# Warm-up matmuls that read a ready-made constant in place of a cleared tile, and three more small ones

## The chip, the cores and the metric

The kernel runs on one core of a Trainium2 chip. The metric is device time in microseconds (us) of one execution. A trace of one execution, taken by the hardware profiler, counts its times from the start of that execution's span; the span is about 1.5 us shorter than the device time. All executions quoted here are of the state "fast". Engines are TensorE (PE in the profile; its weight loads are PEld), VectorE (DVE), ScalarE (ACT), GpSimd (POOL) and SyncE (SP); SPq and ACTq are the DMA queues that SyncE and ScalarE feed. In the views, `arena` is the kernel's own block of on-chip memory and `PS` the accumulator banks that TensorE writes; the weights and x are loaded from HBM, the chip's main memory. A load "lands" when its semaphore says that it is complete.

## The reference, cut to what matters

A layer norm of x (2048 tokens of 512, bf16) feeds two branches whose results are added to x: a diagonal state-space model (a product with B, a scan over tokens, a product with C) and a gated MLP, `(gelu(xn @ w_gate) * (xn @ w_up)) @ w_down`, with a hidden size of 1376. The first thing that TensorE can do of real use is to transpose the first centred tiles of x and multiply them by the first columns of `w_gate` and `w_up`.

## The kernel before: the parts that matter

The kernel builds a list of operations with their buffers, and a scheduler orders them on each engine. TensorE and SyncE keep the order in which they were written down. Before the first real work TensorE runs dummies: seven matmuls of 512 columns and two of 128, then four of 128 between pieces of real work.

```python
half = V(lambda e: e.memset(HALF.ap, 0.5), ...)
wrm = S.order_behind(V(lambda e: e.memset(WRM.ap, 0.0), ...), half)   # the tile the dummies read
...
ld_x0(0)                                        # first x tile, SyncE's queue
S.order_behind(ld_x0(1, "scalar", [wrm]), ...)  # ScalarE's queue, behind wrm
ld_wg0(0, "sync")                               # w_gate columns 0-383, rows 0-255
S.order_behind(ld_wg0(1, "scalar", [wrm]), ...) # rows 256-511
ld_x0(2)
ld_w(WU, WUc, ins["B_w_up"], 0)                 # w_up columns 0-383
ld_x0(3)
...
nwarm = 7
wrm4 = WRM.ap.unsqueeze(1).broadcast_to([128, 4, 128])
def fwarm(e, wb=wb):                            # line 913 of the profile
    for _ in range(nwarm):
        ins_ = e.matmul(PS[wb]..., WRM.ap, wrm4, start=True, stop=True)
PE(fwarm, ..., [WRM], [BANK[wb]], "warm")
def fill(n):                                    # line 920
    ... e.matmul(PS[fb][:, 0:128], WRM.ap, WRM.ap, ...) n times
...
fill(2)
cent_T(0, tb, "AA"); cent_T(1, [wb])            # transposes of x tiles 0, 1: line 673
... w_gate of tile 0, columns 0-383: 8 matmuls  # line 698
fill(4)
...
for r in range(2):
    GT_mm(1, r, ub[1, r], [0])                  # w_gate of tile 1: 8 matmuls
for j in range(2):
    for r in range(2):
        GT_mm(j, r, ub[j, r], [1])              # w_up: needs the B_w_up load
        GT_evac(...)
        if j == 0 and r == 0:
            cent_T(2, tb)                       # transposes of x tile 2: "T2" below
```

(Cuts are marked by dots; comments are mine.)

Of the kernel before, what the change touches and what calls it, by code (L numbers as in the profile page):

```python
# [11 lines left out]
BF16, F32, I32 = dt.bfloat16, dt.float32, dt.int32  # L12
# [349 lines left out]
def d_pe(n_list):  # L362
    return sum(n / 2.4 + 2.5 for n in n_list)
# [9 lines left out]
def build(nc, ins, out):  # L373
    with ExitStack() as es:
# [5 lines left out]
        PS = [E(nc.psum_tensor("PS%d" % i, [128, 512], F32)) for i in range(8)]  # L380
        BANK = [Buf("bank%d" % i, "ps", i, i + 1) for i in range(8)]
# [44 lines left out]
        WRM = A.alloc("WRM", [128], BF16)  # L426
# [47 lines left out]
        PE = lambda fn, dur, r, w, tag="": S.op("tensor", fn, dur, r, w, tag)  # L474
# [82 lines left out]
        def next_bank():  # L557
            b_ = rstate["n"] % 8
            rstate["n"] += 1
            return b_  # L560
# [102 lines left out]
        def cent_T(j, banks, engs="A"):  # L663
            per = KD // len(engs)
            for n, eng in enumerate(engs):
                bank = banks[n]
                pt = PS[bank].bitcast(BF16)

                def f(e, n=n, pt=pt):
                    ins_ = None  # L670
                    for q in range(per):
                        k = per * n + q
                        ins_ = e.transpose(pt[:, 128 * q:128 * (q + 1)], XN[j].ap[:, 128 * k:128 * (k + 1)], IDN.ap)  # L673
                    return ins_
                PE(f, 56.0 * per, [XN[j], IDN], [BANK[bank]], "T0")
                dst = XC_all.ap[:, per * n:per * (n + 1), 128 * j:128 * (j + 1)]
                src = pt[:, 0:128 * per].rearrange("p (q t) -> p q t", q=per)
                w = [XCs[j][n]] if len(engs) == 2 else XCs[j]
                if eng == "A":
                    GATE["evTA"] = ACT(lambda e, src=src, dst=dst: e.activation(dst, src, ACTF.Copy), d_act(128 * per), [BANK[bank]], w, "evT")  # L680
                else:
                    V(lambda e, src=src, dst=dst: e.tensor_copy(dst, src), 110 + 0.6 * 128 * per, [BANK[bank]], w, "evT")
# [221 lines left out]
                    seed(j); hidden(j); states(j); store(j)  # L904

        nwarm = 7
        wrm4 = WRM.ap.unsqueeze(1).broadcast_to([128, 4, 128])
        wb = next_bank()

        def fwarm(e, wb=wb):  # L910
            ins_ = None
            for _ in range(nwarm):
                ins_ = e.matmul(PS[wb][:, :].rearrange("p (a b) -> p a b", a=4), WRM.ap, wrm4, start=True, stop=True)
            return ins_
        PE(fwarm, d_pe([512] * nwarm) * 1.6, [WRM], [BANK[wb]], "warm")
        def fill(n):
            def f(e):
                ins_ = None
                for _ in range(n):
                    ins_ = e.matmul(PS[fb][:, 0:128], WRM.ap, WRM.ap, start=True, stop=True)  # L920
                return ins_
            PE(f, 56.0 * n, [WRM], [BANK[fb]], "fill")

        tb = [next_bank(), next_bank()]
        fb = 7
# [18 lines left out]
        ch(*stats(0, 2)); ch(sub(2))  # L944
        ch(recip(qb0, rq0))

        fill(2)
        cent_T(0, tb, "AA")
        cent_T(1, [wb])
        ub = {(j, r): next_bank() for j in range(2) for r in range(2)}  # L950
# [2 lines left out]
        for r in range(2):  # L953
            GT_mm(0, r, ub[0, r], [0], (2, 3))
        fill(4)
        for j in range(2):
            ch(norms(0, [j], mn0, rq0, 0))
# [65 lines left out]
def bass_parallel_sum__ssm_conv_s5__geglu_ffn__prompt_kernel(  # L1023
    nc: bass.Bass,
    A_x: bass.AP,
    A_Lambda_re: bass.AP,
    A_Lambda_im: bass.AP,
    A_B_re: bass.AP,
    A_B_im: bass.AP,
    A_C_re: bass.AP,  # L1030
    A_C_im: bass.AP,
    A_log_dt: bass.AP,
    A_Dskip: bass.AP,
    B_x: bass.AP,
    B_w_gate: bass.AP,
    B_w_up: bass.AP,
    B_w_down: bass.AP,
    out: bass.AP,
):
    ins = {  # L1040
        "A_x": A_x, "A_Lambda_re": A_Lambda_re, "A_Lambda_im": A_Lambda_im,
        "A_B_re": A_B_re, "A_B_im": A_B_im, "A_C_re": A_C_re, "A_C_im": A_C_im,
        "A_log_dt": A_log_dt, "A_Dskip": A_Dskip,
        "B_w_gate": B_w_gate, "B_w_up": B_w_up, "B_w_down": B_w_down,
    }
    build(nc, ins, out)
# [28 lines left out]
```

## Time and profile before

| | before |
|---|---|
| time, first three runs | 178.35 us median (178.09 to 178.84) |
| span of the traced execution | 177.0 us |
| TensorE busy | 172.5 us, 97% |
| first dummy | 1.02 us |
| first transposes | 4.26 us |
| first matmul that needs the B_w_up load | 7.37 us |

The first part of the page and its fourth part, the chain of waits that ended last, say that TensorE bounds this kernel:

```profile
PE 172.5 (97%) x873; PEld 84.3 (48%) x888; DVE 162.0 (92%) x283; ACT 89.9 (51%) x169; POOL 10.1 (6%) x25
...
PE 94%; DMA 3%; SPq 1%; issue 1%; DVE 0%
```

The same chain in order of time (start, duration, what) shows where it is not TensorE: before 7.37 us, and for the last 0.3 us, VectorE's last addition.

```profile
1.66 0.46 SPq L498
2.16 5.16 DMA arena<-in_B_w_up_dram
7.37 0.50 PE PS L698 x4
7.88 0.22 PE PS L673 x4
8.10 2.32 PE PS L698 x20
```

The timeline of matmuls (start, duration of the group, engine, line, what, count, and in brackets the idle time before it and what ended it):

```profile
1.02 3.17 PE L913 MATMUL PS<-arena 128*128 128x512 bf16 x7 [1.02 <-DVE arena L479]
3.98 0.42 PE L920 MATMUL PS<-arena 128*128 128x128 bf16 x2
4.26 1.03 PE L673 MATMUL PS<-arena 128*128 128x128 bf16 x8
5.22 1.15 PE L698 MATMUL PS<-arena 128*128 128x192 bf16 x8
6.21 0.39 PE L920 MATMUL PS<-arena 128*128 128x128 bf16 x4
6.43 1.45 PE L698 MATMUL PS<-arena 128*128 128x192 bf16 x12
7.71 0.39 PE L673 MATMUL PS<-arena 128*128 128x128 bf16 x4
```

The first dummy is released by VectorE's clear (line 479). The timeline of weight loads, one ahead of each matmul, shows the waits for HBM better, since a weight load is what stands waiting:

```profile
5.86 0.28 PEld L698 LDWEIGHTS PS<-arena 128*128 128x128 bf16 x4 [0.21 <-DMA arena<-in_B_w_gate_dram]
7.37 0.28 PEld L698 LDWEIGHTS PS<-arena 128*128 128x128 bf16 x4 [0.34 <-DMA arena<-in_B_w_up_dram]
```

One more reading matters, the array's rate. Dummies of 512 columns start 0.427 us apart and those of 128 columns 0.107 us. Later the 128-column ones take half of that: the four fillers at 6.21 us start 0.056 us apart. The trace's clock record, which is kept beside the page, opens at 5.85 us, and the spacing of matmuls changes there too. I call this "the switch". The page's own clock row shows 9 from its first slice on and hides it.

### The profile page before, as it was taken

The numbers are of one execution on the slowest core, as the hardware profiler recorded it, in microseconds if no ns is written. First come the engines' busy times: TensorE is split into PE (matmuls) and PEld (weight loads), VectorE is DVE, ScalarE is ACT, GpSimd is POOL, SyncE is SP. The second block draws the span as 40 slices with busy tenths as digits, with TensorE's granted clock in tenths as the row PEclk, the third lists the DMA queues.
The fourth block names the chain that finished last, engine by engine and source line by source line (L and its number), as shares of the span: only waits on it lengthen the run. The fifth ranks groups of instructions, "written<-read, shape, count | busy, mean of one in ns | idle before, by whom it ended". The sixth has DMA issues, their size and how long they took to land.

```text
span 177.0 us, 2494 instructions
## 1 busy us (share of the span) xinstructions
PE 172.5 (97%) x873; PEld 84.3 (48%) x888; DVE 162.0 (92%) x283; ACT 89.9 (51%) x169; POOL 10.1 (6%) x25
## 2 busy tenths in 40 slices
PE   7999999999999999999999999999999999999994
PEld 3854464444644444444644444444454444444453
DVE  6888799997999999879999999999999999999961
ACT  4476378899876899003676792000767780000000
POOL 3222040211000000020000000000000000000000
PEclk9999999999999999999999999999999999999999
DMA  6997987975999000011024000002001000000141
GB/s 151 317 316 100 243 200 162 129 128 113 197 288 224 4 0 2 0 58 60 4 49 99 2 0 0 4 1 88 30 4 25 4 0 0 0 0 0 64 134 44
DMA packets 33396, 14.36 MB, mean 81 GB/s; under 512 B 23688, under 2 KB 33384, under 8 KB 33384
## 3 DMA queue, kind: packets, MB, share of 16 engines
q1 hardware_dynamic: 32944, 13.87, 33.8%
q10 hardware_dynamic: 440, 0.33, 0.7%
q8 instruction: 7, 0.11, 0.3%
q14 instruction: 5, 0.04, 0.1%
HBM read 6.46 MB, written 2.10 MB: 48 GB/s over the span
## 4 chain that ended last, share of the span: by engine, by line
PE 94%; DMA 3%; SPq 1%; issue 1%; DVE 0%
PE PS L864 37%; PE PS L823 32%; PE PS L734 16%; PE PS L698 6%; PE PS L797 3%; DMA arena<-in_B_w_up_dram 3%; SPq L498 0%; PE PS L673 0%; SPq L502 0%; DVE arena L882 0%
## 5 line engine op out<-in xcount | busy, mean ns | idle before, releaser
L864 PE MATMUL PS<-arena 128*128 128x512 bf16 (+3 forms) x317 | 65.9, 366 | 0.3
L823 PE MATMUL PS<-arena 128*128 128x512 bf16 x258 | 57.5, 379 | 0.3
L864 PEld LDWEIGHTS PS<-arena 128*128 128x128 bf16 (+1 forms) x323 | 30.8, 98 | 35.2
L823 PEld LDWEIGHTS PS<-arena 128*128 128x128 bf16 x264 | 25.8, 98 | 30.5
L838 ACT ACTIVATE arena<-PS 128x512 bf16<-128x512 f32 x33 | 19.8, 600 | 37.8 <-PE PS L823 33.1
L767 DVE TENSOR_TENSOR_SCAN arena<-arena 128x512 bf16<-128x512 f32 x32 | 38.8, 1255 | 0.0
L734 PE MATMUL PS<-arena 128*128 128x512 bf16 x125 | 27.8, 379 | 0.2
L842 ACT ACTIVATE arena<-PS 128x512 bf16<-128x512 f32 x33 | 19.8, 599 | 4.3 <-PE PS L823 4.1
L856 ACT ACTIVATE PS<-arena 128x512 f32<-128x512 bf16 (+2 forms) x17 | 9.6, 581 | 20.4 <-PE PS L864 19.7
L734 PEld LDWEIGHTS PS<-arena 128*128 128x128 bf16 x128 | 12.5, 98 | 14.9 <-issue 0.2
L738 ACT ACTIVATE arena<-PS 128x512 bf16<-128x512 f32 x32 | 17.5, 594 | 2.1 <-PE PS L734 2.1
L882 DVE TENSOR_TENSOR arena<-PS,arena 128x512 bf16<-128x512 f32 (+2 forms) x17 | 10.9, 654 | 5.0 <-PE PS L864 4.5
L844 DVE TENSOR_TENSOR arena<-arena 128x512 bf16<-128x512 bf16 x33 | 13.0, 418 | 1.5 <-ACT arena L842 1.4
L698 PE MATMUL PS<-arena 128*128 128x192 bf16 (+2 forms) x80 | 13.3, 321 | 0.1
L624 DVE BATCH_NORM_STATS2 arena<-arena 128x6 f32<-128x512 bf16 x16 | 10.3, 684 | 2.3 <-DMA arena<-in_A_x_dram 2.3
L698 PEld LDWEIGHTS PS<-arena 128*128 128x128 bf16 x80 | 7.2, 99 | 5.3 <-DMA arena<-in_B_w_up_dram 0.3
L756 DVE TENSOR_TENSOR arena<-arena 128x4096 bf16<-128x4096 bf16 (+1 forms) x5 | 9.2, 1861 | 0.2 <-ACT arena L620 0.2
L707 ACT ACTIVATE arena<-PS,arena 128x192 bf16<-128x192 f32 (+1 forms) x16 | 6.7, 447 | 5.3 <-PE PS L698 3.6
L779 DVE TENSOR_TENSOR arena<-arena 128x4096 bf16<-128x4096 bf16 x4 | 9.2, 2291 | 0.1
L754 DVE TENSOR_TENSOR arena<-arena 128x4096 bf16<-128x4096 bf16 (+1 forms) x5 | 9.2, 1860 | 0.0
L780 DVE TENSOR_TENSOR arena<-arena 128x4096 bf16<-128x4096 bf16 x4 | 9.1, 2286 | 0.0
L710 DVE SCALAR_TENSOR_TENSOR arena<-PS,arena 128x192 bf16<-128x192 f32 (+1 forms) x16 | 6.6, 443 | 0.6 <-ACT arena L707 0.6
(84 smaller groups left out, 110.1 us busy)
## 6 DMA issues: line engine op xcount, KB each, us to landing
out_dram<-arena SPq DMA_DIRECT2D x15, 128.0 KB, 1.7
arena<-in_A_x_dram SPq DMA_DIRECT2D x3, 512.0 KB, 5.3
arena<-in_B_w_down_dram SPq DMA_DIRECT2D x1, 1280.0 KB, 7.9
arena<-in_B_w_gate_dram SPq DMA_DIRECT2D x2, 256.0 KB, 5.7
arena<-in_B_w_up_dram SPq DMA_DIRECT2D x2, 256.0 KB, 5.9
arena<-in_B_w_gate_dram SPq DMA_DIRECT2D x1, 480.0 KB, 5.9
arena<-in_B_w_up_dram SPq DMA_DIRECT2D x1, 480.0 KB, 5.9
arena<-arena SPq DMA_TRANSPOSE x25, 2.6
```

Of the source, the lines that this page charges most:

```text
L624: return (V(lambda e: e.bn_stats(ST[tt].ap, X[tt].ap), d_dve_1x(512), [X[tt]], [ST[tt]], "bnst"), V(lambda e: e.bn_aggr(MVt[b][j].ap, ST[t ...
L698: ins_ = e.matmul(dst, XCd(j, k), WGU[:, us[0]:us[-1] + 1, k, f0:f1], start=(k == 0), stop=(k == KD - 1))
L734: ins_ = e.matmul(PS[bank][:, :], BBT[c][dk].ap[:, 128 * s:128 * (s + 1)], XNT[b].ap[:, dk, :], start=(dk == 0), stop=(dk == KD - 1))
L738: GATE["evBu"] = ACT(lambda e, bank=bank, k3=k3, s=s, c=c: e.activation(SSc[k3][s][c].ap, PS[bank][:, :], ACTF.Copy), d_act(512), [BANK[ba ...
L767: V(lambda e, g=g, rb=rb, init=init: e.tensor_tensor_scan(g.ap, rb, g.ap, init, ALU.mult, ALU.add), d_dve_scan(512), [g, PA[RRr]] + ([CARc ...
L823: ins_ = e.matmul(PS[bank][0:m, c0:c1], W.ap[:, dk, 128 * ft:128 * ft + m], XNT[b].ap[:, dk, c0:c1], start=(dk == 0), stop=(dk == KD - 1))
L838: GATE["last_gelu"] = ACT(lambda e, bg=bg, kk=kk, m=m: e.activation(GG[kk].ap[0:m, :], PS[bg][0:m, :], ACTF.Gelu_apprx_tanh), d_act(512), ...
L842: ACT(lambda e, bu=bu, kk=kk, m=m: e.activation(UPB[kk].ap[0:m, :], PS[bu][0:m, :], ACTF.Copy), d_act(512), [BANK[bu]], [UPB[kk]], "evU")
L844: V(lambda e, kk=kk, m=m, ft=ft, k2=k2: e.tensor_tensor(HTt[k2][ft].ap[0:m, :], GG[kk].ap[0:m, :], UPB[kk].ap[0:m, :], ALU.mult), d_dve_tt ...
L856: ACT(lambda e: e.activation(PS[bank][:, c0:c1], X[tt].ap[:, c0:c1], ACTF.Copy), d_act(c1 - c0), [X[tt]], [BANK[bank]], "seed")
L864: ins_ = e.matmul(PS[bank][:, c0:c1], l_[:, 128 * j:128 * (j + 1)], r_[:, c0:c1], start=False, stop=last and n == len(ops) - 1, skip_group ...
L882: V(lambda e: e.tensor_tensor(OUTB[ko].ap[:, c0:c1], PS[bank][:, c0:c1], XD[tt].ap[:, c0:c1], ALU.add), d_dve_1x(c1 - c0), [BANK[bank], XD ...
```

## The change

The intent: the dummies are there to have TensorE at its full rate earlier (without them, in no_dummies below, the switch came at 6.99 us and the kernel took some 1 us longer). They wait for VectorE's clear although a constant that the framework fills in at 0.31 us, ahead of the start barrier, would do. So the dummies read that constant and can start right after the barrier, and three more fillers keep TensorE busy until the first transposes.

```diff
-        wrm4 = WRM.ap.unsqueeze(1).broadcast_to([128, 4, 128])
+        ones, ones4 = nc.const_aps.tensor(1.0, (128, 128), BF16), nc.const_aps.tensor(1.0, (128, 512), BF16)
...
-                ins_ = e.matmul(PS[wb][:, :].rearrange("p (a b) -> p a b", a=4), WRM.ap, wrm4, start=True, stop=True)
+                ins_ = e.matmul(PS[wb][:, :], ones, ones4, start=True, stop=True)
...
-        PE(fwarm, d_pe([512] * nwarm) * 1.6, [WRM], [BANK[wb]], "warm")
+        PE(fwarm, d_pe([512] * nwarm) * 1.6, [], [BANK[wb]], "warm")
...
-                    ins_ = e.matmul(PS[fb][:, 0:128], WRM.ap, WRM.ap, start=True, stop=True)
+                    ins_ = e.matmul(PS[fb][:, 0:128], ones, ones, start=True, stop=True)
...
-            PE(f, 56.0 * n, [WRM], [BANK[fb]], "fill")
+            PE(f, 56.0 * n, [], [BANK[fb]], "fill")
...
-        fill(2)
+        fill(5)
```

The order of instructions on the other four engines stays the same. VectorE still clears the tile, since two loads are ordered behind it.

## The prediction

> **What bounds the kernel now.** TensorE. The page's first part has it busy 172.5 of 177.0 us (97%); the chain of waits gives it 94% of the span. The rest of that chain lies at the front: SyncE issues loads from 0.74 us, the load of B_w_up issued at 2.16 us takes 5.16 us (3%), and at 7.37 us the first matmuls that use it (line 698) start; from there the chain is matmuls to within 0.5 us of the last work. So nothing that TensorE does before 7.37 us is on the chain: in the timeline of weight loads it stands idle 0.34 us before 7.37 us and 0.21 us before 5.86 us, for two loads from HBM.
>
> **What the change does.** The seven 512-column dummies start at 1.02 us, released by VectorE's clear of their tile (0.85 us, 0.11 us long). The constant is filled by GpSimd at 0.31 us, before the start barrier, after which ScalarE's first work is at 0.73 us. I expect the first dummy at about 0.77 us: 0.25 us earlier. The dummies run cold, 0.427 us apart for 512 columns and 0.107 us for 128. Three more small ones add 0.32 us, so the fillers end at 0.77 + 2.99 + 0.54 = 4.30 us against 4.20 now. The first transposes need VectorE's subtraction, done at 4.20, and start at 4.26 us; they may slip 0.05 us, hidden before the 5.86 us load. VectorE still clears the tile, as two loads are ordered behind it. Order on the other engines is unchanged. [...]
>
> **Where a gain could come from.** Only the clock. [...] spacing of 192-column matmuls drops from 0.160 to 0.082 us at 5.86 us, 4.8 us after the first dummy (the page's clock row, 9 throughout, hides the cold start). [...] Estimate from the trace's durations: the work between 5.86 and 7.37 us has 0.28 us of slack and each cold microsecond costs 0.5, so switches before about 6.4 us cost nothing [...] Expected gain 0.05 us, 0.03%; [...]
>
> **Prediction.** 178.3 us, range 177.9 to 178.8. Faster by over 2%: 0.005; within 2%: 0.99; slower by over 2%: 0.005.
>
> **What would show it.** First dummy near 0.77 us with no VectorE releaser; transposes at 4.26 to 4.31 us; the chain still through the load of B_w_up, landing near 7.3 us; a switch of rate anywhere before 6.4 us leaves the time unchanged. Times keep a spread of some 0.7 us with a floor near 178.1.
>
> **What would make it wrong.** [...] TensorE leaving the barrier later than I think; or loads landing differently from run to run.

The forecast's sum came to a gain of 0.05 us: 178.3 us against the median of 178.35 us before. The 0.05 us can't be worked out again. Two of the risks in the last paragraph rested on the same figure and are cut too, as is a remark on ones in place of zeros. (On the latter the traces show that the large dummies start 0.427 us apart with either.)

## The result, and the profile after

The changed kernel took 178.22 us (median of 6, 177.83 to 178.81), the kernel before 178.39 us in the 6 runs compared with it (178.00 to 178.84). The ratio is 0.9994, with a 95% interval from 0.9971 to 1.0016: the same. (A ratio is the mean time of one kernel's fast runs over that of the other's of the same rounds, so it is not quite the ratio of the medians.)

The page's first part and its chain, of the traced execution of 176.6 us:

```profile
PE 173.4 (98%) x891; PEld 84.9 (48%) x891; DVE 162.4 (92%) x283; ACT 90.3 (51%) x169; POOL 10.3 (6%) x25
...
PE 98%; DVE 0%; issue 0%
```

The chain in order of time now begins with the dummies and never waits for another engine or a load until the last addition:

```profile
0.78 3.15 PE PS L913 x7
3.92 0.53 PE PS L920 x5
4.46 0.85 PE PS L673 x8
5.31 1.01 PE PS L698 x8
6.32 0.23 PE PS L920 x4
6.55 0.99 PE PS L698 x12
7.54 0.22 PE PS L673 x4
```

The timeline of matmuls, and after it the timeline of weight loads, in which no wait for a load is left:

```profile
0.78 3.15 PE L913 MATMUL PS<-const-bfloat16-1.0 128*128 128x512 bf16 x7 [0.78 <-PEq L1060]
3.71 0.74 PE L920 MATMUL PS<-const-bfloat16-1.0 128*128 128x128 bf16 x5
4.25 1.06 PE L673 MATMUL PS<-arena 128*128 128x128 bf16 x8
7.38 0.39 PE L673 MATMUL PS<-arena 128*128 128x128 bf16 x4
```

```profile
4.19 0.85 PEld L673 LDWEIGHTS PS<-arena 128*128 128x128 bf16 x8
5.21 0.88 PEld L698 LDWEIGHTS PS<-arena 128*128 128x128 bf16 x8 [0.16 <-issue]
6.07 0.30 PEld L920 LDWEIGHTS PS<-const-bfloat16-1.0 128*128 128x128 bf16 x4
6.33 0.98 PEld L698 LDWEIGHTS PS<-arena 128*128 128x128 bf16 x12
```

The first dummy is 0.24 us earlier and the transposes start where they did. The switch came at 5.81 us, where it had come at 5.85. The four transposes of x tile 2 (I call their start T2) came at 7.38 us instead of 7.71. That difference of 0.33 us is nearly all of the 0.35 us between the two spans, but nothing shows it to be the change's doing. B_w_up landed at 7.33 us in one execution and at 6.87 us in the other, and both loads were issued at about the same time (2.16 and 2.17 us) behind the same loads. Over the eleven traces with this order of loads it landed at 6.96 to 7.88 us where the dummies read the cleared tile (three traces) and at 6.87 to 7.67 us in the other eight: the ranges overlap, and so few draws can't exclude that the change moves the landing. Two traces of single executions could easily be told as a story of an earlier start that pays 0.3 us. The interval above is too wide to contradict it (0.9971 would be 0.5 us); the pooled times further down do.

### The profile page after: what moved, and what is told of

The parts are those of the page before. It is cut to its first block, busy times and chain, and to the rows that moved or that the text cites. A ratio compares the mean times of both kernels' runs of the same rounds, so it can differ in the third digit from the quotient of the medians.

```text
span 176.6 us, 2515 instructions
## 1 busy us (share of the span) xinstructions
PE 173.4 (98%) x891; PEld 84.9 (48%) x891; DVE 162.4 (92%) x283; ACT 90.3 (51%) x169; POOL 10.3 (6%) x25
## 4 chain that ended last, share of the span: by engine, by line
PE 98%; DVE 0%; issue 0%
PE PS L864 37%; PE PS L823 32%; PE PS L734 16%; PE PS L698 7%; PE PS L797 3%; PE PS L913 2%; PE PS L673 1%; PE PS L920 0%; DVE arena L882 0%
## 5 line engine op out<-in xcount | busy, mean ns | idle before, releaser
L823 PE MATMUL PS<-arena 128*128 128x512 bf16 x264 | 58.1, 379 | 0.0
L734 PE MATMUL PS<-arena 128*128 128x512 bf16 x128 | 28.1, 379 | 0.0
```

The source lines that it names most:

```text
L734: ins_ = e.matmul(PS[bank][:, :], BBT[c][dk].ap[:, 128 * s:128 * (s + 1)], XNT[b].ap[:, dk, :], start=(dk == 0), stop=(dk == KD - 1))
L823: ins_ = e.matmul(PS[bank][0:m, c0:c1], W.ap[:, dk, 128 * ft:128 * ft + m], XNT[b].ap[:, dk, c0:c1], start=(dk == 0), stop=(dk == KD - 1))
```

## The experiments

In the traces of both kernels 166.75 us pass from T2 to the end of the last matmul (7.71 to 174.47 and 7.38 to 174.13). So the question became what sets T2. My theory (A) said that the loads do, unless the switch comes late. The rivals were: (B) the earlier start brings a real gain through an earlier switch; (C) the switch is tied to the program's start, whatever the dummies do. Each run below is timed against the kernel before in the same rounds (the rounds ran on three chips), and its trace gives one more draw of the switch and of the landings. Switch and landing times are from the trace's clock record and landing records.

### The changed kernel again

No edit.

> The changed kernel once more, for a second trace and a tighter interval. Theory A (the front is hidden: the matmuls that need the B_w_up load at about 7.0 to 7.3 us wait for it, or reach it just as it lands, so the dummies' start does not matter while the switch to full rate comes before about 6.4 us): ratio to before 0.9990 to 1.0005. Theory B (the earlier start brings a real gain by an earlier switch): ratio 0.998 or less. On the switch itself: [...] if it is tied to the program's start it is again near 5.8 us; if it follows the first dummy by a fixed time it is at 5.8 here and was at 5.85 in before though the dummy came 0.24 us later there, which already speaks against it.

Measured: ratio 1.0000 (0.9986 to 1.0014), 178.19 us median: within A's band, and against a B of 0.998 or less. In this execution the switch came at 6.52 us and T2 at 7.72 us, with B_w_up landed at 6.96 us and no wait for it. So the same kernel reached T2 0.34 us later because the switch came 0.71 us later: 0.48 us per us.

### The constant alone, and the three fillers alone

```diff
# const_only, against the changed kernel
-        fill(5)
+        fill(2)
# fill5_only, against the kernel before
-        fill(2)
+        fill(5)
```

> The constant alone, two small fillers as before. First dummy at 0.78 us, fillers end near 3.93 us instead of 4.25, so TensorE idles about 0.3 us until the transposes at 4.26 us. Theory A: ratio to before 0.999 to 1.001, switch not later than 6.4 us. [...]

> The three fillers alone, the dummies still on the cleared tile. First dummy at 1.02 us, fillers end near 4.52 us, so the transposes start 0.26 us late. Theory A: hidden before the loads, since the work up to the B_w_up load has 0.28 us of slack: ratio 0.999 to 1.002. If the front is not hidden but TensorE itself is the chain from its first dummy on: 0.26 us longer, ratio 1.0015 or more.

Measured: const_only 1.0018 (1.0001 to 1.0035), 178.57 us median; fill5_only 1.0028 (1.0005 to 1.0050), 178.74 us median. Both intervals lie above 1, that of const_only by a hair, and both ratios lie outside theory A's bands (up to 1.001 and 1.002); that of fill5_only is in the rival's, in which TensorE itself is the chain from its first dummy on. So neither part alone is faster than before, and the fillers alone cost. The trace of fill5_only shows the transposes pushed to 4.51 us, as expected, but also an execution whose gate load landed late, at 6.85 us, where other traces with this order of loads have 5.0 to 5.8. Here is its timeline of weight loads:

```profile
5.47 0.45 PEld L698 LDWEIGHTS PS<-arena 128*128 128x128 bf16 x4 [0.16 <-issue]
6.89 0.28 PEld L698 LDWEIGHTS PS<-arena 128*128 128x128 bf16 x4 [0.98 <-DMA arena<-in_B_w_gate_dram]
8.37 0.29 PEld L673 LDWEIGHTS PS<-arena 128*128 128x128 bf16 x4
```

After the wait the work ran at full rate, and T2 came at 8.45 us, 1.60 us after that landing. The four runs of const_only average 0.33 us above before, which I can't explain: its one trace (switch at 5.98 us, T2 at 7.50 us) is of its fastest run. The rival that is cut from its expectation rested on a figure that no run of this case shows; it was that the gap before the transposes delays the switch. That is not seen in this trace: the gap is 0.45 us between weight loads, and the switch came at 5.98 us, between the 5.81 and 6.52 us of the changed kernel. Nor did a longer idle time prevent it: below, in no_dummies, TensorE had nothing to do before 4.25 us and the switch came 2.74 us later.

### No dummies before the transposes

```diff
-        PE(fwarm, d_pe([512] * nwarm) * 1.6, [], [BANK[wb]], "warm")
...
-        fill(5)
```

> No dummies before the transposes: TensorE's first work at about 4.26 us. [...] cold work from 5.85 on costs 0.5 us per us less 0.28 us of slack, so 0.7 to 2.4 us longer, ratio 1.004 to 1.013. If the dummies are worth nothing: ratio 1.000.

Measured: 1.0062 (1.0038 to 1.0086), 178.74 to 179.75 us in four runs. The dummies are worth some 1 us. The traced execution, the fastest of the four, had the switch at 6.99 us, only 2.74 us after its first matmul at 4.25 us, earlier than I had allowed. (The 0.7 to 2.4 us and the ratio were my estimate only.)

### The dummies later

```diff
-        nwarm = 7
+        nwarm = 3
...
-        PE(fwarm, d_pe([512] * nwarm) * 1.6, [], [BANK[wb]], "warm")
+        PE(fwarm, d_pe([512] * nwarm) * 1.6, [IDN], [BANK[wb]], "warm")
```

> The changed kernel with its dummies released 1.58 us later (by VectorE's identity tile, ready at 2.33 us) and four large dummies fewer, so that the fillers end at the same 4.2 us. A dose of the suspected cause 6.5 times the 0.24 us of the change, in the other direction. [...] the time is longer by some 0.3 to 0.8 us, ratio 1.002 to 1.0045; from that the 0.24 us of the change are worth a sixth, 0.05 to 0.12 us. If the switch is tied to the program's start (seen so far at 5.8 to 7.0 us in six traces, even 6.99 without dummies): again 5.8 to 7.0 us and a ratio of 1.000 to 1.001.

Measured: 1.0039 (1.0014 to 1.0064); means 178.95 against 178.28 us. The first dummy was at 2.39 us and the switch at 7.41 us, 5.02 us later; the ratio is in the band expected if the dummies' start matters (1.002 to 1.0045; the band was my estimate only). T2 came at 8.15 us with no wait for a load:

```profile
5.23 1.09 PEld L698 LDWEIGHTS PS<-arena 128*128 128x128 bf16 x8 [0.16 <-issue]
6.33 0.52 PEld L920 LDWEIGHTS PS<-const-bfloat16-1.0 128*128 128x128 bf16 x4
6.81 1.27 PEld L698 LDWEIGHTS PS<-arena 128*128 128x128 bf16 x12
8.07 0.29 PEld L673 LDWEIGHTS PS<-arena 128*128 128x128 bf16 x4
```

Compare these groups with those of the changed kernel: the same eight, four and twelve weight loads take 1.09, 0.52 and 1.27 us instead of 0.88, 0.30 and 0.98. So the start of the dummies does matter, against C, and it has a price: against before, 1.37 us later cost 0.67 us, 0.49 us per us (by the ratio's interval 0.18 to 0.83). At that price the change's 0.24 us are worth 0.12 us (0.04 to 0.20). The price is one of start and number together, since four of the seven large dummies went too. Without dummies the first work came 3.23 us later than before's first dummy and cost 0.95 us, 0.30 per us, which would make 0.07 us (0.05 to 0.11).

### The B_w_up load earlier, and later

```diff
# up_early, against the changed kernel
-        ld_x0(2)
         ld_w(WU, WUc, ins["B_w_up"], 0)
+        ld_x0(2)
         ld_x0(3)
# up_late
         ld_x0(2)
-        ld_w(WU, WUc, ins["B_w_up"], 0)
         ld_x0(3)
+        ld_w(WU, WUc, ins["B_w_up"], 0)
```

> The changed kernel with the B_w_up load issued before the third x tile, so that it lands about 0.4 us earlier (6.5 to 6.9 us). Theory: the start of the transposes of tile 2 (7.38 to 7.72 us in the traces, 166.75 us before the last matmul's end in each of them) is the later of two things, the landing of B_w_up plus 0.38 us and TensorE's own path, which the clock's switch sets. Then this takes away only the first: 7.3 to 7.7 us by the switch, ratio to before 0.998 to 1.000, and no wait before the matmuls that use the load. If the load alone bound the front: 0.4 us shorter, ratio 0.9977. The later x tile could delay the norms and cost instead.

> The changed kernel with the B_w_up load issued after the fourth x tile, landing about 0.4 us later (7.3 to 7.7 us). By the theory of the later of two, the load bounds nearly every execution now: the transposes of tile 2 at 7.7 to 8.1 us, TensorE idle 0.3 us or more before them, ratio to before 1.001 to 1.003. If TensorE's cold path alone bound the front: ratio 1.000.

Measured: up_early 1.0081 (1.0053 to 1.0108), a miss in direction; up_late 1.0010 (0.9990 to 1.0030). In up_early's trace, of the slowest of its four runs, B_w_up landed at 7.78 us and so not earlier at all, the gate load at 6.80 us, and x tile 2 only at 8.22 us, so that VectorE centred it late:

```profile
6.84 0.28 PEld L698 LDWEIGHTS PS<-arena 128*128 128x128 bf16 x4 [1.12 <-DMA arena<-in_B_w_gate_dram]
9.60 0.23 PEld L673 LDWEIGHTS PS<-arena 128*128 128x128 bf16 x4 [1.26 <-DVE arena L932]
```

I had taken the landing of one load as something that can be moved alone. In the one trace there is, it couldn't. The chain of that trace runs through x tile 2, which was issued 0.5 us later than in the other kernels; the gate load was issued before the exchanged loads, and fill5_only's landed as late without any exchange. In up_late the load landed at 7.15 us, within the range of the kernels with the old order (6.87 to 7.88 us), and T2 came at 7.55 us with no wait for it: the expected wait of 0.3 us was not there, and 0.47 us of later issue did not show as a later landing.

### Without the four fillers between the real work

```diff
-        fill(4)
```

> The changed kernel without the four fillers after the first eight matmuls of real work. They take 0.23 us of TensorE's path at full rate and 0.43 at half. Where TensorE's path binds, up to 0.23 us is won; where the load binds, nothing. By the theory of the later of two: 0.05 to 0.2 us shorter than the changed kernel, ratio to before 0.9985 to 0.9997. If the fillers are needed to bring the clock up: slower, switch later than 7 us.

Measured: 1.0011 (0.9987 to 1.0035), no gain seen. The trace caught the earliest switch of all, at 4.01 us, and TensorE then stood waiting for B_w_up, which landed at 6.94 us:

```profile
4.24 0.49 PEld L673 LDWEIGHTS PS<-arena 128*128 128x128 bf16 x8
6.99 0.28 PEld L698 LDWEIGHTS PS<-arena 128*128 128x128 bf16 x4 [0.61 <-DMA arena<-in_B_w_up_dram]
```

T2 was 7.33 us, hardly earlier than in the changed kernel's first trace (7.38), though the switch came 1.8 us earlier. The eight transposes (line 673), here after the switch, took 0.49 us of weight loads; in the changed kernel's first trace, before the switch, they took 0.85 us.

### The load taken off the path

The first four w_up units compute with w_gate's columns, which are there already, and do not wait for B_w_up (a wrong result; order and traffic unchanged).

```diff
-    ... WGU[:, us[0]:us[-1] + 1, k, f0:f1], ...
+    ... WGU[:, 0:1, k, f0:f1] if us == [1] else WGU[:, us[0]:us[-1] + 1, k, f0:f1], ...
+    # and these four units leave out their wait for the B_w_up load
```

> The kernel before, with its first four B_w_up units computed from B_w_gate's columns instead (a wrong result on purpose), so that TensorE first needs the B_w_up load about 1.3 us later; order of instructions and traffic unchanged. Theory (the start of the transposes of tile 2 is the latest of: TensorE's own path, 7.38 us + 0.48 for each us that the switch comes after 5.81; the landing of B_w_gate's second half + 1.6; the landing of B_w_up + 0.38): the third term goes, so no wait for B_w_up before those transposes, and they start at 7.38 + 0.48 x (switch - 5.81) us, unless the gate load lands after 5.85. Ratio to before 0.9985 to 0.9998, since in the trace of before the load cost 0.31 us. If the load is not what binds: 1.000.

> The changed kernel with the same relief. If the B_w_up load is what hid the change's gain, this is faster than the relieved kernel before by 0.48 x 0.24 = 0.1 us or more; the ratio to before 0.998 to 0.9992. If the change's gain is small because the switch's phase spreads over 3 us whatever the dummies do, the two relieved kernels still agree within 0.2 us.

Measured: the kernel before with this edit 0.9994 (0.9975 to 1.0014), mean 178.35 us; the changed kernel with it 0.9987 (0.9971 to 1.0003), mean 178.23 us. The difference of 0.12 us is what the price above gives, and within the noise. In free_before's trace the switch came at 4.22 us, and by the terms of TensorE's path and of the gate load (landed at 5.49 us) T2 should have come at 7.1 us; it came at 7.47 us, because the next thing in line was not ready, VectorE's centred x tile 2:

```profile
7.47 0.23 PEld L673 LDWEIGHTS PS<-arena 128*128 128x128 bf16 x4 [0.44 <-DVE arena L932]
```

So in this execution a very early switch was not worth more, even without the load.

### A candidate, and the changed kernel a third time

The B_w_up load in two halves by rows; eight matmuls that need only the first half go first; no fillers between:

```diff
-        ld_w(WU, WUc, ins["B_w_up"], 0)
+        ld_wu0(0); ld_wu0(1)          # rows 0-255, rows 256-511
...
-        fill(4)
...
-                GT_mm(j, r, ub[j, r], [1])
+                GT_mm(j, r, ub[j, r], [1], (0, 1))
+        for j in range(2):
+            for r in range(2):
+                GT_mm(j, r, ub[j, r], [1], (2, 3))
```

> A candidate to beat both, correct: the changed kernel with the B_w_up load in two halves by rows, the four units that need it in two passes, eight matmuls that need only the first half ahead of those that need the second, and no fillers between. Landing of the last half then has 8 x 0.08 us more to hide under. If the front is as the theory says, 0.1 to 0.3 us shorter than the changed kernel: ratio to before 0.9980 to 0.9992. It may lose by another order on VectorE, which the scheduler rearranged: then the work after the transposes of tile 2 is no longer 166.75 us long.

> The changed kernel a third time, for its mean and one more trace of the switch: ratio to before 0.9985 to 1.001, [...] transposes of tile 2 by the later-of-three rule within 0.05 us.

Measured: split_after 1.0017 (0.9991 to 1.0042), no gain: T2 came at 7.92 us with the switch at 6.40 us, and TensorE waited 0.42 us for ScalarE at 8.99 us. The changed kernel's third run gave 0.9983 (0.9965 to 1.0001), with the switch at 6.37 us and T2 at 7.64 us. No version that I tried beats both kernels.

### What sets T2

The traces together give a rule: T2 is the latest of (1) TensorE's own path, 7.38 us + 0.48 for each us of the switch after 5.81; (2) the gate load's landing + 1.60; (3) B_w_up's landing + 0.38; and (4) x tile 2 out of VectorE. The constants come from after and after_again (1), fill5_only (2) and before (3). The other six rows test (1) and (3); no row tests the 1.60 of (2).

| trace | first dummy | switch | gate landed | B_w_up landed | rule | T2 | what binds |
|---|---|---|---|---|---|---|---|
| before | 1.02 | 5.85 | 5.82 | 7.33 | 7.71 | 7.71 | B_w_up |
| after | 0.78 | 5.81 | 5.45 | 6.87 | 7.38 | 7.38 | TensorE |
| after_again | 0.77 | 6.52 | 5.64 | 6.96 | 7.72 | 7.72 | TensorE |
| after_third | 0.77 | 6.37 | 5.30 | 7.06 | 7.65 | 7.64 | TensorE |
| const_only | 0.78 | 5.98 | 5.03 | 7.11 | 7.49 | 7.50 | both |
| fill5_only | 1.02 | 6.61 | 6.85 | 7.88 | 8.45 | 8.45 | gate load |
| no_dummies | none | 6.99 | 5.26 | 6.91 | 7.95 | 7.92 | TensorE |
| late_start | 2.39 | 7.41 | 5.70 | 7.67 | 8.15 | 8.15 | TensorE |
| up_late | 0.77 | 6.15 | 5.23 | 7.15 | 7.54 | 7.55 | both |
| no_mid_fill | 0.77 | 4.01 | 5.23 | 6.94 | 7.32 | 7.33 | B_w_up |

From T2 to the end of the last matmul it is 166.75 or 166.76 us in all ten. Three traces stand outside: free_before and up_early are bound by x tile 2 (4), and split_after has another order. In free_after the trace has no clock record; matmul spacing puts the switch near 5.1 us, for which the rule gives 7.04, and T2 was 7.13. The straight line of (1) is only shown from 5.8 us on. So theory A, that the loads set T2 unless the switch is late, does not hold as I had it: in five of the ten traces TensorE's own path is the last, in two it ties with the load, in three a load is the last.

## Why the prediction was right

- **The time.** Predicted 178.3 us, 177.9 to 178.8; measured 178.22. Right, but "no change", 178.35 us, would have been as near: the number alone tests no mechanism. Pooled over all series and chips, the changed kernel has a mean of 178.22 us (18 runs, 177.83 to 178.81) and the kernel before 178.32 (39 runs, 177.78 to 178.97, one of its four series without the changed kernel). The difference is 0.10 us, with about 0.15 either way (two standard errors of the two means), so a gain is likely and not shown.
- **The first dummy** at about 0.77 us, released by no VectorE work: 0.78 us. **The transposes** at 4.26 to 4.31 us: 4.25 us. Right.
- **"The chain still through the load of B_w_up"**: wrong. It was so in the trace of before, and not in that of after, because the load landed 0.46 us earlier there. Of the traces of the two kernels (one and three), only that of before is bound by the load.
- **"Only the clock"**: supported as far as the traces go. The switch came at 4.01 to 7.41 us, in kernels with the same start of dummies at 4.01 (no_mid_fill), 5.81, 6.37 and 6.52 us. After the first matmul it came 2.74 us (no_dummies) to 5.75 us (after_again) later. So in these traces its moment is fixed neither by the program's start nor by the first matmul; what fixes it is not shown. A switch tied to the program's start is contradicted by that spread, and a start of the dummies without effect by late_start and no_dummies.
- **"Switches before about 6.4 us cost nothing"**: the step that was mis-sized. I took the slack of 0.28 us from one trace, in which the load happened to land late (7.33 us). In after_again the load landed at 6.96 us, there was no slack, and a switch at 6.52 us cost 0.34 us against one at 5.81; the prediction has 0.06 us for that. So a cold microsecond cost its 0.48 us from 5.8 us on in most of the traced executions, and the change's expected gain, an estimate by the doses of no_dummies and late_start, is 0.07 to 0.12 us where the prediction had 0.05. With the intervals given above the doses allow 0.04 to 0.20 us, and the direct comparison can't tell 0.05 from 0.12 either.
- **The spread** of some 0.7 us with a floor near 178.1: the spread of before was 1.2 us over 39 runs, with a floor of 177.78. The moment of the switch is only one of its causes; the landings of the loads are another (in the ten traces of the table TensorE's own path is last in five and a load in three).

What stays open: why const_only averaged 0.33 us above before, why loads of the same order land up to 1.8 us apart (the gate load, at 5.03 to 6.85 us over the eleven traces), what decides the moment of the switch, and whether the change itself saves 0.1 us.

## What to carry to other kernels

When a kernel is bound by one engine almost from the start, look for the moment from which the rest is of constant length, and ask what sets that moment: here it is the latest of four things, at least three of which (the switch and two landings) differ from execution to execution. A small step in one of them is paid only in the executions in which that one is last, so cost it over several traces and not from one trace's slack. Where the step itself is too small to measure, move the same cause by a multiple in the other direction: the dummies 1.37 us later gave a price of 0.49 us per us, if a rough one, that the 0.24 us of the change could not.
